# Converting a second weight matrix later inside a fused mLSTM and Fourier-mix kernel

## The chip, the cores and the metric

The kernel runs on one core of one Trainium2 chip. The metric is the device time of one execution in microseconds (us), lower is better. Three runs of the kernel before gave a median of 402.24 us (402.18 to 402.57). One execution was also profiled; every duration below comes from that one.

## What is computed

An mLSTM cell runs over 4 batches, 8 heads, 768 tokens and 40 features a head. Its output, reshaped to (4, 768, 320), goes through a Fourier mix and a two-layer MLP:

```python
for t in range(S):                       # attention part
    m_new = np.maximum(f_gate[:, :, t] + m, i_gate[:, :, t])
    ...
    C = f_stab * C + i_stab * np.einsum('bhd,bhe->bhde', vt, kt)
    h_tilde = np.einsum('bhde,bhe->bhd', C, qt)
    ...
    y[:, :, t] = o * h_tilde / denom
X = np.fft.fft(np.fft.fft(x, axis=1), axis=2)    # second part, x = y reshaped
u = x + np.real(X)
un = (u - mu) / np.sqrt(var + 1e-06)
ch = np.maximum(un @ w_ch1, 0.0) @ w_ch2          # 320 -> 1280 -> 320
return u + ch
```

The two weight matrices arrive as 64-bit floats. The kernel reads them as 64-bit words and turns them into 32-bit floats by itself, and that conversion is what the change moves.

## The kernel before, in words

**Order of the work.** The whole program is laid out by hand in numbered slots. `at(slot, phase, fn, ...)` puts a call into a plan, and `run` (line 127) emits the calls sorted by slot and phase. Within a slot the phases are EVAC = 0, FILL = 1, MAIN = 2 and FILL_PE = 3, with fractions for the order inside one. A slot is not a stretch of time that the chip knows: it only fixes the order in which each engine gets its instructions. Each engine works through its own instructions in that order and waits, where it must, for another engine's result.

**Batches.** Four batches overlap (lines 1331 to 1335). While batch 0 is in its MLP (`mlp_in`, slots 31 to 50, the first layer; `mlp_out`, slots 51 to 62, the second), batch 1 is in its recurrence (`plan_halves`, line 762). That recurrence has six chunks of 128 tokens. Chunk c starts at slot 32 + 3c, so a period of the recurrence is three slots. The text calls a step of it by batch and chunk, as in (1,2).

**A chunk of the recurrence**, with s = 32 + 3c (lines 762 to 788):
- ScalarE: exponentials of half the heads (`mlstm_exp`, line 491) in slot s-1 and the other half in slot s
- TensorE, slot s: scores (`halves_scores`) and the sums for the state (`halves_to_state`) into one PSUM bank pair, which has a single copy
- VectorE: `halves_add` (lines 665, 667), the state's two halves, in slots s+1 and s+2 ahead of everything else there; `halves_weigh` (line 672) in slot s+1. Both read the bank pair, so the next chunk's scores wait for them
- GpSimd: `halves_decay` (line 652), the scaled queries (line 501), the mask (line 515), the weighted values (line 507)
- TensorE, slot s+3: `halves_from_state`, then `halves_from_chunk` with turn 0, and after the next chunk's scores `halves_from_chunk` with turn 1. Between the two turns ScalarE makes a one-element copy, `halves_between` (line 699, tile `warm`), for which turn 1 waits
- VectorE, slot s+4: `mlstm_finish` (lines 712 to 720).

**A piece of the weights** (class `Piece`, lines 382 to 427) is 128 x 640 numbers. There are ten, n = 0 to 9: 0 to 4 are the first matrix, 5 to 9 the second. Each goes through four steps: `load` (line 396, 640 KB on SyncE's queue into tile `raw`, two buffers), `take` (lines 406 and 408, VectorE, tiles `e` and `m`, one buffer each), `convert` (lines 413 and 414, ScalarE, two instructions) and `join` (lines 420, 422 and 426, VectorE). The load of piece n waits for the join of piece n-2, the take of n for the join of n-1. Lines 1342 to 1351 put the steps into the plan: each triple in `when` is the slot and phase of take, convert and join.

**Who needs the pieces.** `mlp_in` for blocks 4 and 5 (slots 35 and 36) is the first to read pieces 3 and 4. `mlp_out` reads pieces 5 to 7 in slot 51 and pieces 7 to 9 in slot 52. `weight_sums` (line 1081) reuses the tiles `raw`, `e` and `m` from slot 52 on.

**Other work in these slots.** `mix_add` (line 937) on VectorE adds the Fourier part for batch 0 (slots 31, 35, 36), `mix_center` (line 971, tile `uc`) and `mix_turn_out` (line 983) on ScalarE follow it, with TensorE's transposes (line 978, tile `put`) between them. After every second block of `mlp_in`, ScalarE runs two `mlp_relu` (line 1071).

The steps of pieces 3 to 9 stand in these slots before:

| piece | take | convert | join |
|---|---|---|---|
| 3 | 22 | 23 | 27 |
| 4 | 27 | 28 | 32 |
| 5 | 33 | 34 | 34 |
| 6 | 34 | 35 (after TensorE's work of the slot) | 36 |
| 7 | 36 | 37 | 38 |
| 8 | 39 | 40 | 41 |
| 9 | 42 | 43 | 44 |

Of the kernel before, what the change touches and what calls it, by code (L numbers as in the profile page):

```python
# [53 lines left out]
def kernel(  # L54
# [1285 lines left out]
    at(60, FILL + 0.4, lambda: nc.gpsimd.memset(ds_sb[0:1, 0, 0, :], 1.0))  # L1340

    when = [((2, 0.7), (4, 0.5), (6, 0.6)), ((6, 0.7), (7, 0.5), (8, 0.6)), ((11, 0.7), (13, 0.5), (22, 0.6))]
    when += [((22, 0.7), (23, 0.7), (27, 0.6)), ((27, 0.7), (28, 0.7), (32, 0.6))]
    when += [((33, 0.7), (34, 0.3), (34, 0.6)), ((34, 0.7), (35, 2.7), (36, 0.6))]
    when += [((s, 0.7), (s + 1, 0.7), (s + 2, 0.6)) for s in (36, 39, 42)]
    pieces = w1_pieces + w2_pieces
    for n, (w, p) in enumerate(zip(when, pieces)):
        if n > 4:
# [138 lines left out]
```

## Time and profile before

| what | value |
|---|---|
| median of three runs | 402.24 us |
| the profiled execution's own time | 402.53 us |
| its span in the trace | 400.8 us |
| TensorE busy (matmul) | 382.8 us, 96% |
| VectorE busy | 279.8 us, 70% |
| ScalarE busy | 171.7 us, 43% |
| GpSimd busy | 132.6 us, 33% |
| mean granted TensorE clock | 0.991 |

The span is what the trace covers; the other 1.73 us of the profiled execution lie around it. In the trace's names PE is TensorE's matmuls, PEld its weight loads, DVE VectorE, ACT ScalarE, POOL GpSimd and SP SyncE, whose queue issues the transfers. A timeline line gives start, duration, engine, line of the kernel, operation, names of what is written and read, shapes and count; a bracket at its end is the idle time of that engine just before and what ended it. In this program a float matmul leaves two records, so `x8` on line 1056 is four matmuls of the first layer.

The matmuls of `mlp_in` begin at 59.18 us, those of `mlp_out` at 117.65 us. The stretch between them is where slots 31 to 50 run.

### The profile page before, as it was taken

The page shows a single profiled execution, that of the slowest core. Times are in us where ns is not written, and L with a number is a line of the kernel's source. Part 1 is how long each engine was busy: PE and PEld are TensorE (multiplying, and loading weights), DVE is VectorE, ACT ScalarE, POOL GpSimd, SP SyncE. Part 2 cuts the span into 40 slices and gives each one's busy share as a digit, 9 for nine tenths or more (in the row PEclk, how much of TensorE's full clock was granted, in tenths as well). Part 3 has the DMA queues.
Part 4 walks back from the last instruction along what each step waited for, and adds up shares of the span by engine and source line. Part 5 has one row for each costly group of instructions (what it writes and reads, how often), then busy time and mean ns, then how long its engine had stood idle before and what let it go on. Part 6 is the DMA issues. An engine that isn't in the chain of part 4 may idle for free.

```text
span 400.8 us, 10588 instructions
## 1 busy us (share of the span) xinstructions
PE 382.8 (96%) x4174; PEld 278.4 (69%) x4174; DVE 279.8 (70%) x671; ACT 171.7 (43%) x481; POOL 132.6 (33%) x237
## 2 busy tenths in 40 slices
PE   8999899979999999998999989989999999999996
PEld 6877555545567677755569888845578986556996
DVE  7789988999665467485775598777764686336652
ACT  6987367655640232655462214544440023454000
POOL 5648513555863341253255124451310000020000
PEclk9999999979999999999999999999999999999999
DMA  7878499677286254447800526410000000000100
GB/s 222 288 228 246 151 241 275 191 191 220 72 190 169 60 155 127 118 133 185 186 1 28 138 71 194 145 38 2 0 0 18 17 34 33 2 0 0 34 33 34
DMA packets 25631, 44.78 MB, mean 112 GB/s; under 512 B 5727, under 2 KB 14766, under 8 KB 25454
## 3 DMA queue, kind: packets, MB, share of 16 engines
q1 hardware_dynamic: 25582, 44.11, 39.1%
q8 instruction: 33, 0.54, 0.6%
q14 instruction: 16, 0.13, 0.1%
HBM read 38.49 MB, written 4.12 MB: 106 GB/s over the span
## 4 chain that ended last, share of the span: by engine, by line
PE 67%; DVE 18%; DMA 6%; issue 4%; ACT 2%; POOL 1%; SPq 1%; DVEq 0%; POOLq 0%; ACTq 0%
PE po L1237 18%; PE pm L1118 14%; PE po L1181 8%; PE pm L1056 5%; PE ph L519 4%; PE pm L1123 4%; PE pu L935 3%; PE ps L519 2%; DMA Gb<-G_d 2%; DVE so L716 2%; DMA raw<-in_w 1%; PE pz L904 1%; PE pz L892 1%; DMA W<-M_d 1%; PE put L978 1%
## 5 line engine op out<-in xcount | busy, mean ns | idle before, releaser
L1187 DVE SCALAR_TENSOR_TENSOR x<-po,rstd,x 128x160 f32<-128x160 f32 (+1 forms) x69 | 27.0, 395 | 43.9 <-PE po L1237 36.8
L1127 DVE TENSOR_TENSOR h<-h,pm 128x384 f32<-128x384 f32 x60 | 30.5, 550 | 29.2 <-PE pm L1123 13.9
L652 POOL TENSOR_TENSOR C<-C,decB 128x164 f32<-128x164 f32 x30 | 16.0, 532 | 75.7 <-DVE C L667 64.7
L1118 PE MATMUL pm<-uT,w_sb 128*128 128x384 f32 x90 | 37.7, 506 | 2.1 <-DVE h L1127 1.3
L491 ACT ACTIVATE W<-W,colT 128x64 f32<-128x64 f32 x144 | 37.4, 339 | 0.0
L1181 PE MATMUL po<-w_sb,h 128*128 128x320 f32 x120 | 34.2, 435 | 0.0
L1056 PE MATMUL pm<-uT,w_sb 128*128 128x384 f32 x80 | 31.2, 528 | 0.3 <-DVE x L955 0.2
L515 POOL TENSOR_SCALAR_AFFINE_SELECT W<-W 64x512 f32<-64x512 f32 x36 | 27.2, 756 | 11.7 <-ACT W L491 10.4
L1002 POOL TENSOR_TENSOR t<-rstd 128x6 f32<-128x6 f32 x12 | 3.4, 281 | 81.9 <-DVE v L996 81.4
L1237 PE MATMUL po<-T,S 128*128 128x160 f32 x180 | 27.9, 302 | 1.5 <-DVE x L1187 1.5
L501 POOL TENSOR_TENSOR qg<-qk,Gb 128x512 f32<-128x512 f32 (+1 forms) x21 | 28.7, 1368 | 1.4 <-DMA kvt<-in_kv 0.8
L1181 PEld LDWEIGHTS po<-w_sb,h 128*128 128x128 f32 x120 | 22.3, 190 | 9.5 <-issue 0.6
L1237 PEld LDWEIGHTS po<-T,S 128*128 128x128 f32 x180 | 25.5, 190 | 3.2 <-DVE x L1187 2.0
L1118 PEld LDWEIGHTS pm<-uT,w_sb 128*128 128x128 f32 x90 | 15.5, 189 | 16.4 <-DVE h L1127 7.5
L1237 PE MATMUL po<-w_sb,h 128*128 128x160 f32 x180 | 26.3, 300 | 0.0
L1237 PEld LDWEIGHTS po<-w_sb,h 128*128 128x128 f32 x180 | 25.2, 190 | 1.4 <-DVE x L1187 0.3
L1174 ACT ACTIVATE h<-h 128x384 f32<-128x384 f32 x45 | 23.1, 520 | 2.0 <-DVE h L1127 2.0
L1123 PE MATMUL pm<-uT,w1t_sb 64*128 64x384 f32 x120 | 23.4, 508 | 0.0
L983 ACT COPY uT<-put 128x384 f32<-128x384 f32 x24 | 11.1, 476 | 27.5 <-PE put L978 27.5
L1056 PEld LDWEIGHTS pm<-uT,w_sb 128*128 128x128 f32 x80 | 15.0, 202 | 11.0 <-issue 3.2
L507 POOL TENSOR_TENSOR vw<-kvt,colT 128x328 f32<-128x328 f32 x23 | 18.0, 782 | 12.7 <-DVE colT L360 10.1
L971 ACT ACTIVATE uc<-x 128x384 f32<-128x384 f32 x24 | 14.4, 613 | 18.1 <-DVE x L963 12.1
(241 smaller groups left out, 843.3 us busy)
## 6 DMA issues: line engine op xcount, KB each, us to landing
kvt<-in_kv SPq DMA_DIRECT2D x24, 336.0 KB
qk<-in_qkT SPq DMA_DIRECT2D x48, 160.0 KB
raw<-in_w SPq DMA_DIRECT2D x10, 640.0 KB
Gb<-G_d SPq DMA_DIRECT2D x36, 128.0 KB
W<-M_d SPq DMA_DIRECT2D x36, 128.0 KB
so<-in_o SPq DMA_DIRECT2D x24, 160.0 KB
out<-x SPq DMA_DIRECT2D x24, 160.0 KB
x<-so SPq DMA_DIRECT2D x9, 140.0 KB
```

The lines of the kernel that those rows point to most:

```text
L491: nc.scalar.activation(out=k.W[:, h, :], in_=M, func=AF.Exp, scale=-1.0, bias=colT[:, c, 0, b * H + h:b * H + h + 1])
L501: nc.gpsimd.tensor_tensor(out=k.qg[:, :, t], in0=k.qk[:, 0, :, t], in1=k.Gb[:, :, t], op=OP.mult)
L515: nc.gpsimd.affine_select(out=W, in_=W, compare_op=OP.is_ge, fill=0.0, base=base, pattern=[[0, H], [step, LH]], channel_multiplier=-1)
L519: nc.tensor.matmul(out, w, x, start=start, stop=True, skip_group_check=True)
L1056: nc.tensor.matmul(k.pm[i], w1_sb[:, ch, f0:f0 + L], u[2 * ch], start=(ch == 0 and not ahead), stop=(ch == 1 and ahead), skip_group_check= ...
L1118: nc.tensor.matmul(bank, w, u, start=start, stop=True, skip_group_check=True)
L1123: nc.tensor.matmul(bank, block(w1t_sb, i)[rows], mlp_u(gr, 1)[rows], start=False, stop=True, skip_group_check=True)
L1127: nc.vector.tensor_tensor(out=h, in0=h, in1=bank, op=OP.add)
L1174: nc.scalar.activation(out=h, in_=h, func=AF.Relu, scale=-1.0)
L1181: nc.tensor.matmul(k.po, hidden(gr, f)[:, i * L:(i + 1) * L], w2_sb[:, f, :], start=(f == 0), stop=(f == NFF - 1))
L1187: nc.vector.scalar_tensor_tensor(out=u, in0=po, scalar=k.rstd[:, c:c + 1], in1=u, op0=OP.mult, op1=OP.add)
L1237: nc.tensor.matmul(po, a[:, f], w[:, f], start=start and f == 0, stop=f == half - 1, skip_group_check=True)
```

## The change

Only the table `when` changes. Piece 3 is joined in slot 31 and no longer in 27. With it piece 4 moves: it is taken in slot 31, converted in 32 and joined in 33. Pieces 5 to 9 follow at three-slot steps, from slots 36, 39, 42, 45 and 48, each with its convert one slot and its join two slots after the take. The last join is now in slot 50 and no longer in 44. The loads of pieces 5 to 9 move too, since line 1349 puts the load of piece n one slot after the join of piece n-2: from slots 28, 33, 35, 37, 39 to 32, 34, 39, 42, 45. No instruction is added or taken away.

```diff
     when = [((2, 0.7), (4, 0.5), (6, 0.6)), ((6, 0.7), (7, 0.5), (8, 0.6)), ((11, 0.7), (13, 0.5), (22, 0.6))]
-    when += [((22, 0.7), (23, 0.7), (27, 0.6)), ((27, 0.7), (28, 0.7), (32, 0.6))]
-    when += [((33, 0.7), (34, 0.3), (34, 0.6)), ((34, 0.7), (35, 2.7), (36, 0.6))]
-    when += [((s, 0.7), (s + 1, 0.7), (s + 2, 0.6)) for s in (36, 39, 42)]
+    when += [((22, 0.7), (23, 0.7), (31, 0.5)), ((31, 0.7), (32, 0.7), (33, 0.6))]
+    when += [((s, 0.7), (s + 1, 0.7), (s + 2, 0.6)) for s in (36, 39, 42, 45, 48)]
     pieces = w1_pieces + w2_pieces
     for n, (w, p) in enumerate(zip(when, pieces)):
         if n > 4:
             at(when[n - 2][2][0] + 1, FILL + 0.7, p.load)
         for (s, phase), fn in zip(w, (p.take, p.convert, p.join)):
             at(s, FILL + phase, fn)
```

## The prediction

> **What bounds the kernel now.** I read the page's slices first. TensorE is busy nearly everywhere, and its granted clock falls in one slice of ten us only, the ninth (80 to 90 us).
>
> ```profile
> PE   8999899979999999998999989989999999999996
> PEclk9999999979999999999999999999999999999999
> ```
>
> Next I read the list of waits of TensorE between 56 and 125 us, the stretch in which pieces 3 to 9 are handled. It is short: 3.6 us in four waits (columns: total, times, longest).
>
> ```profile
> PE ps L519 <- DVE C L667: 1.9, 1, 1.9
> PE ph L519 <- ACT warm L699: 1.1, 1, 1.1
> PE put L978 <- ACT uc L971: 0.4, 1, 0.4
> PE pm L1056 <- DVE x L955: 0.2, 1, 0.2
> ```
>
> TensorE's timeline places the two long ones, and shows that the first layer's next eight records take 4.63 us where the same group takes 2.85 us at 99.20:
>
> ```profile
> 83.82 0.69 PE L519 MATMUL ps<-qk 40*64 40x64 f32 x32 [1.86 <-DVE C L667]
> 84.33 0.70 PE L519 MATMUL ps<-vw,kvt 64*40 64x41 f32 x32
> 86.17 0.66 PE L519 MATMUL ph<-kvt,W 64*64 64x41 f32 x16 [1.13 <-ACT warm L699]
> 86.76 0.90 PE L978 MATMUL put<-ident,uc 128*128 128x128 f32 x3
> 87.46 4.63 PE L1056 MATMUL pm<-uT,w_sb 128*128 128x384 f32 x8
> ...
> 99.20 2.85 PE L1056 MATMUL pm<-uT,w_sb 128*128 128x384 f32 x8
> ```
>
> The table of windows says why (the clock is the 0.50 ahead of the DMA share): after the waits the clock is halved until about 91.1 us.
>
> ```profile
> 83.00:84.00 1.00, 0.18 (x11) 0.18 (x14) 0.76 (x3) 0.84 (x2) 0.16 (x1) 1.00 0.57 113
> 88.00:89.00 1.00, 1.00 (x3) 0.60 (x2) 0.66 (x4) 1.00 (x4) 0.92 (x2) 0.50 0.77 232
> ```
>
> Last, the chain of work that ended last, in order of time, names what TensorE waited for. The join of piece 6 and the take of piece 7 run ahead of the state's add on VectorE, and the convert of piece 7 runs ahead of the exponentials and `warm` on ScalarE:
>
> ```profile
> 80.27 0.73 DVE e L420
> ...
> 81.78 0.84 DVE w_sb L426
> ...
> 82.64 0.50 DVE e L406
> ...
> 83.16 0.43 ACT e L413
> ...
> 83.90 0.72 ACT m L414
> 84.62 0.95 ACT W L491 x4
> ...
> 86.08 0.05 ACT warm L699
> ```
>
> So this spot is bound by the weights' conversion on VectorE and ScalarE; from 87.46 to 126 us TensorE has no wait at all, though VectorE idles there only about 6 us in all, the longest being:
>
> ```profile
> 105.59 0.33 DVE L667 TENSOR_TENSOR C<-C,ps 128x164 f32<-128x164 f32 x1 [1.72 <-POOL C L652]
> 111.95 0.33 DVE L667 TENSOR_TENSOR C<-C,ps 128x164 f32<-128x164 f32 x1 [2.74 <-PE ps L519]
> ```
>
> **What the Trainium skill says.** "TensorE: Matmul & The Clock Gate", Part 1, has the clock drop to half after an idle window of about 3.4 us and return after a busy one. The trace agrees roughly: 1.86 and 1.13 us of waiting, with some 1.2 us of work between, and then 0.50 for about 6.7 us. "GPSIMD Engine Reference", section 8, says that GpSimd shares SBUF interfaces with VectorE and contends with its two-input instructions. The trace agrees: line 422 takes 0.82 us at 80.92 with GpSimd idle and 1.88 us at 84.91 under GpSimd's line 501.
>
> **The change, part by part.** Times named "before" are starts in the trace.
>
> *Slots 27 to 36, VectorE.* From 57.91 (join 3) to 83.45 (the late add) VectorE runs four joins and four takes; after the change joins 3 and 4 and takes 4 and 5. What leaves is joins 5 and 6 (0.81 + 1.08 + 1.77 and 0.81 + 0.82 + 0.82) and takes 5 and 6 (0.57 + 1.02 and 0.83 + 0.94): 9.5 us, and a 1.32 us wait for a transfer. Joins 3 and 4 come later but in time: batch 0's add of slot 31 goes first (58.0 to 59.15), join 3 ends near 61.6, take 4 near 62.4, and join 4, behind its convert and the first add of (1,0), near 66.9. Blocks 4 and 5 read those pieces at 70.95 and 74.96, so 4 us or more cover it.
>
> *ScalarE there.* With take 4 at 61.6 the exponentials of (1,0) run first and `uc` at about 64.4 instead of 65.86, so TensorE's 0.44 us wait for `put` at 66.52 goes. VectorE now waits for TensorE: the add of (1,1) follows at about 74.4 (before 75.89), and the 3.70 us from there to the weigh (75.89 to 79.59) put that at 78.1. The 0.16 us wait at 77.45 goes too.
>
> *Slots 36 to 38.* After the weigh (0.60) comes take 5 (0.81), then the second add, done at 79.8. TensorE wants it at 81.95 - 0.6 = 81.35: the 1.86 us go with 1.5 us to spare. ScalarE's convert 5 runs 79.1 to 80.5, exponentials to 81.5, `uc` to 82.05, `warm` at 82.15; turn 1 wants it at 82.3. The 1.13 us go, with almost nothing to spare. No idle, no halved clock: 4.63 becomes 2.85 (1.8), and the transposes and small products at half clock give about 0.7 (0.90, 0.66 and 0.70 against 0.55, 0.42 and 0.50). Sum: 0.44 + 0.16 + 1.86 + 1.13 + 1.8 + 0.7 = 6.1 us, all on TensorE's path.
>
> *Slots 39 to 50, where it is given back.* Here come joins 6, 7, 8 and takes 7, 8, 9 in place of joins 8, 9 and take 9 (join 9 falls at the end). VectorE keeps the old spacing: weigh to weigh was 10.94 us with join 6 in it. Less that join (2.45) and its waits of 0.26 and 0.47 it is 7.76, so the weigh of (1,2) is at 85.9. From there to that of (1,4) was 90.53 to 108.29 = 17.76 with two pieces in it; less the 0.37 us wait for TensorE that is 17.4, so 103.2. TensorE asks for it at 110.75 - 6.1 = 104.65: in time. But take 8 follows it (103.8), convert 8 waits for take 8 (104.3 to 105.7), and behind convert 8 on ScalarE stand two `mlp_relu` (0.8), four exponentials (1.0) and `warm` (0.1): 107.6. Turn 1 of (1,4) wants that at 111.63 - 6.1 = 105.5. A new wait of 2.1 us. It is between 1.2 (take 8 without contention and a join 0.5 shorter) and 3.0 (take 8 as slow as take 6, 1.77).
>
> *Slot 50 on.* Join 8 starts near 105.3 and takes 2.45 to 3.96 (the joins of 101.45 and 92.51); with add 0.25 and finish 1.65 to 2.05 the weigh of (1,5) ends at 110.3 to 112.2. TensorE wants it at 115.24 - 4.0 = 111.2: 0 to 1.0, I take 0.2. Join 9 follows the fold of slot 50 (1.6, from 114.89 to 116.5 before) and ends at 116 to 117.5; block 8 of `mlp_out` reads it at 117.65 - 3.8 + 2.69 + 1.6 = 118.1. Covered by 0.6 us or more; if not, it costs what it is late. VectorE's 3.09 us idle at 123.43 then takes up its lag.
>
> *Loads.* Each still waits on SyncE's queue for a join, with exponent inputs and `so` behind it. Load 5 waits for join 3 (about 61), load 7 for join 5 (about 83). Each lands well before its take, some 10 us later; before, take 5 waited 1.32 us. Cost zero; if the cover failed, about 1.3 us a piece.
>
> Sum: -6.1 + 2.1 + 0.2 = -3.8 us. The profiled execution of 402.53 us (span 400.8 and 1.73 around it) goes to 398.7; it lies 0.29 above the median, so the median of 402.24 goes to **398.4**.
>
> **Rivals.** (1) *Nothing comes back*: GpSimd leaves VectorE alone, take 8 is done before 101.7, `warm` is in time: -6.1, 396.1 us. For it: GpSimd is 33% busy. Against: the 8.7 us old spacing, and GpSimd's chain ahead of the add at 105.59.
> (2) *More comes back*: the 2.1 us wait joins the scores' wait in slot 47 and the clock halves again, 1.8 to 2 us: 400.4. For it: 3.0 us of waiting did it before. Against: 2.1 is shorter.
> (3) *Slower: VectorE becomes the bound of slots 39 to 50.* The weigh of (1,5) is at 78.1 plus four periods P. Before it was in time at 114.3, with 0.3 to spare, so beyond P = 9.1 us the kernel loses. I have P = 8.1. With joins and takes stretched by GpSimd throughout as the worst were (line 422 1.89, line 426 1.77, take 1.77), P nears 9.5: 78.1 + 38.0 = 116.1, 1.5 us late, and the halved clock 1.8: 405.5. Against: the two measured periods with a whole piece were 8.73 and 9.03, waits included.
> (4) *No net effect*: another result is late at 81.35 and the old wait stays under a new name; 402.2. Against: GpSimd's results for (1,1) were there in time.
>
> **How the numbers follow.** About 0.2% (0.8 us) is what a measurement can tell from no change. Forecast (397.2 to 399.8) 0.50; (1) 0.15; (2) 0.20; (4) 0.05; (3) 0.10. Faster: 0.50 + 0.15 + 0.20 = 0.85; same 0.05; slower 0.10. The range 396.2 to 401.2 takes in the forecast, (2) and half of (1), about 0.8.
>
> **What would show it.** Right: no waits near 82 to 86, the clock whole in the ninth slice, first layer's eight records 2.85 us there; a wait for `warm` of about 2 us in slot 47, near 106; `mlp_out` starting near 113.9 instead of 117.65, and the same 3.8 us at the end. Wrong: a clock below 1 between 80 and 125, a wait for a weigh (line 672) or join (line 426) over 1 us, or a later gap that takes back what `mlp_out`'s start gained.

## The result and the profile after

| what | before | after |
|---|---|---|
| median of five runs | 402.24 us | 400.46 us |
| the profiled execution's own time | 402.53 us | 400.47 us |
| its span | 400.8 us | 398.8 us |
| start of `mlp_in`, of `mlp_out` in the trace | 59.18, 117.65 us | 59.48, 115.50 us |
| ratio after to before, 95% interval | | 0.9943 [0.9923, 0.9963] |

By the medians the kernel is 1.78 us faster; the forecast was 3.8. The ratio is one of means and stands for 2.3 us, between 1.5 and 3.1. (Two runs further down, of the changed kernel once more and of the last experiment, each had one execution of 542 us at a mean clock of 0.66, which their ratios leave out.) The page's slices show that the dip of the clock has not gone: it has moved, from the ninth slice to the twelfth, and is shallower.

```profile
PE   8999899999899999998999989989999999999996
PEclk9999999999989999999999999999999999999999
```

The list of TensorE's waits between 56 and 125 us is down from 3.6 to 2.5 us (columns: total, times, longest):

```profile
PE ph L519 <- ACT warm L699: 2.2, 2, 1.7
PE put L978 <- ACT uc L971: 0.3, 1, 0.3
```

TensorE's timeline places them. In slot 38 a small rest of the old waits is left and the eight records that took 4.63 us take 2.75. In slot 47 there is a new wait, and behind it eight records of the same kind take 4.54 us, where before they took 2.85 (at 111.98):

```profile
82.42 0.44 PE L519 MATMUL ph<-kvt,W 64*64 64x41 f32 x16 [0.50 <-ACT warm L699]
...
83.18 2.75 PE L1056 MATMUL pm<-uT,w_sb 128*128 128x384 f32 x8
...
107.76 0.44 PE L519 MATMUL ph<-kvt,W 64*64 64x41 f32 x16 [1.74 <-ACT warm L699]
108.13 4.54 PE L1056 MATMUL pm<-uT,w_sb 128*128 128x384 f32 x8
```

The table of windows gives the granted clock there, again the figure ahead of the DMA share. It is whole until 109 and then 0.50 until past 112.

```profile
106.00:107.00 1.00, 0.02 (x4) 0.00 (x0) 1.00 (x2) 1.00 (x4) 1.00 (x2) 1.00 0.03 5
110.00:111.00 1.00, 1.00 (x3) 0.66 (x2) 0.96 (x2) 0.00 (x0) 0.79 (x3) 0.50 0.92 203
```

The chain of work that ended last, in order of time, runs through the same kinds of steps as before the change, now with piece 8: the weigh of (1,4), take 8, convert 8, the rectifiers, the exponentials and the one-element copy.

```profile
102.92 0.69 DVE W L672
103.62 0.88 DVE e L406
...
104.52 0.76 ACT e L413
...
105.88 0.85 ACT h L1071 x2
106.73 0.95 ACT W L491 x4
107.67 0.04 ACT warm L699
```

Two intervals of the traces give the balance. From the start of `mlp_in` to the tail matmuls of block 9 (92.02 before, 85.85 after) TensorE gained 32.84 - 26.37 = 6.5 us. From there to the start of `mlp_out` it lost 29.65 - 25.63 = 4.0 us. Of that, 2.1 us lie between the state product of (1,4) and turn 1 (1.36 us before, 3.48 after), 1.7 us in the halved clock (4.54 against 2.85), and 0.2 us are spread over the stretch before slot 47. What is left, 2.45 us, is 2.15 us in the trace's own times because `mlp_in` began 0.30 us later. That start lies anywhere between 58.54 and 60.13 us in the traces of this case, with no order by the change.

### The profile page after: what moved, and what is told of

Read it like the earlier page. It is cut to its first block, busy times and chain, and to the rows that moved or that the text cites. A ratio compares the mean times of both kernels' runs of the same rounds, so it can differ in the third digit from the quotient of the medians.

```text
span 398.8 us, 10582 instructions
## 1 busy us (share of the span) xinstructions
PE 382.2 (96%) x4174; PEld 278.0 (70%) x4174; DVE 279.4 (70%) x671; ACT 171.8 (43%) x481; POOL 134.6 (34%) x237
## 4 chain that ended last, share of the span: by engine, by line
PE 66%; DVE 17%; DMA 6%; issue 4%; ACT 3%; POOL 2%; SPq 1%; DVEq 0%; POOLq 0%; ACTq 0%
PE po L1237 18%; PE pm L1118 14%; PE po L1181 8%; PE pm L1056 3%; PE pm L1123 3%; PE pu L935 3%; PE ph L519 3%; PE ps L519 2%; DMA kvt<-in_kv 2%; PE put L978 2%; DMA Gb<-G_d 1%; DMA raw<-in_w 1%; PE pz L904 1%; PE pz L892 1%; DMA qk<-in_qkT 1%
## 5 line engine op out<-in xcount | busy, mean ns | idle before, releaser
L501 POOL TENSOR_TENSOR qg<-qk,Gb 128x512 f32<-128x512 f32 (+1 forms) x21 | 27.6, 1316 | 0.1
L507 POOL TENSOR_TENSOR vw<-kvt,colT 128x328 f32<-128x328 f32 x23 | 18.9, 820 | 13.0 <-DVE colT L360 10.1
```

Source lines behind the costliest of these rows:

```text
L501: nc.gpsimd.tensor_tensor(out=k.qg[:, :, t], in0=k.qk[:, 0, :, t], in1=k.Gb[:, :, t], op=OP.mult)
```

## The experiments

The theory: the gain is real, and what came back comes from VectorE's work of the weights, now crowded into slots 39 to 50, through the take and convert that stand in front of the copy `warm`. There are three rivals: VectorE is simply too slow there; or GpSimd's chain in front of VectorE's add is the cause; or the joins of pieces 3 and 4 made the gain. The edits below are made to the changed kernel, unless they say otherwise. Each ratio is to the kernel before, run beside it. The changed kernel itself, run once more, gave this:

> The changed kernel itself once more, beside the two others on the same chip. Both theories: ratio to before 0.993 to 0.997; the wait for the one-element copy in slot 47 at 1.6 to 1.9 us. It settles how much of the difference to the other runs lies in the chip.

Measured: 0.9929 [0.9903, 0.9955], 400.42 us, the wait in slot 47 at 1.7 us. The first measurement holds.

**Each part alone.** First only pieces 5 to 9 moved, then only pieces 3 and 4:

```diff
-    when += [((22, 0.7), (23, 0.7), (31, 0.5)), ((31, 0.7), (32, 0.7), (33, 0.6))]
+    when += [((22, 0.7), (23, 0.7), (27, 0.6)), ((27, 0.7), (28, 0.7), (32, 0.6))]
```

> Only pieces 5 to 9 stand as in the changed kernel; pieces 3 and 4 stand as before the change. Theory (the waits near 82 and 86 went because pieces 5 and 6 left slots 33 to 36): both stay away, the wait for the transposed block of 0.4 us near 66 comes back, the wait in slot 47 stays as in the changed kernel: 400.5 to 401.0. Rival (pieces 3 and 4 matter, they let the additions of batch 0 run first): a wait for the state's add near 82 comes back, 402 or more.

Measured: 0.9953 [0.9935, 0.9970], 401.16 us. The wait near 82 stays away and the one near 86 is down to 0.49 us; the 0.4 us for the transposed block is back; the wait in slot 47 is 1.74 us. This is as the theory had it; the median lies 0.16 us above its range.

```diff
-    when += [((s, 0.7), (s + 1, 0.7), (s + 2, 0.6)) for s in (36, 39, 42, 45, 48)]
+    when += [((33, 0.7), (34, 0.3), (34, 0.6)), ((34, 0.7), (35, 2.7), (36, 0.6))]
+    when += [((s, 0.7), (s + 1, 0.7), (s + 2, 0.6)) for s in (36, 39, 42)]
```

> Only pieces 3 and 4 stand as in the changed kernel (joins in slots 31 and 33); pieces 5 to 9 stand as before the change, so that slots 31 to 36 hold joins 3 to 6 and takes 4 to 7. Theory (the gain comes from pieces 5 and 6 leaving those slots): VectorE is as late at the state's second add of (1,1) as before, the waits near 82 and 86 and the halved clock stay: ratio to before 0.998 to 1.003. Rival (joining 3 and 4 later is what helps): the waits near 82 are gone, ratio about 0.990.

Measured: 1.0028 [1.0014, 1.0041]: slower than before. Its list of waits has the two long old ones again:

```profile
PE ps L519 <- DVE C L667: 1.9, 1, 1.9
PE ph L519 <- ACT warm L699: 1.3, 1, 1.3
PE put L978 <- ACT uc L971: 1.1, 1, 1.1
```

The 1.1 us for the transposed block lies at 76.69; a wait of 0.8 us stands at the same block, at 77.74, in the trace of the kernel before with a later Newton step (below). So the gain belongs to pieces 5 and 6 leaving slots 33 to 36. Joining 3 and 4 later without that costs a little. The likely reason is that it adds to the crowd, but the trace, of one of the fastest of 22 executions, does not show it.

**Taking one step out of the chain to the copy.** Convert 8 behind the copy:

```diff
+    when[8] = ((45, 0.7), (47, 2.65), (48, 0.6))
```

> Convert 8 moves on ScalarE from slot 46 to slot 47 behind the one-element copy, join 8 to slot 48; nothing else moves. Theory (the 1.74 us wait of TensorE in slot 47 comes from convert 8, which waits for take 8 and holds back the rectifiers, exponentials and the copy): that wait is under 0.4 us, the clock stays whole, the second layer starts near 112.0 instead of 115.5; join 9 then ends near 117.5 and block 8 of the second layer may wait 1 to 1.5 us for it, so 1.9 to 3.5 us less than the changed kernel: 397.0 to 398.5. Rival (VectorE as a whole is too slow in slots 39 to 50, whatever stands on ScalarE): a wait of about the same size turns up in slots 47 to 50 for the weigh, 400 to 401.

Measured: 0.9942 [0.9926, 0.9957]. The wait in slot 47 is gone, as the theory says, but the time is not better: convert 9, which waits for take 9, stands in front of the copy of slot 50.

```profile
113.82 0.53 PE L519 MATMUL ph<-kvt,W 64*64 64x41 f32 x16 [2.25 <-ACT warm L699]
```

That copy is hardly later than in the changed kernel (54.3 us after the start of `mlp_in`, there 54.2). There TensorE, held up in slot 47, reached it late; here it comes early and waits. The clock halves behind this wait, and the first 30 records of `mlp_out` take 9.89 us instead of 8.34.

Take 8 ahead of the weigh, right behind join 7:

```diff
+    when[8] = ((44, 0.7), (46, 0.7), (47, 0.6))
```

> Only take 8 moves, from slot 45 behind the weigh of (1,4) to slot 44 right behind join 7, into the 1.73 us in which VectorE idles for GpSimd. Theory: convert 8 is then ready before the rectifiers need ScalarE, TensorE's wait for the copy in slot 47 goes, the clock stays whole; join 8 still stands ahead of the weigh of (1,5), for which TensorE may wait up to 1 us in slot 50: 397.0 to 398.8. Rival (VectorE too slow as a whole): the wait moves to the weigh of (1,5) in full and the clock halves anyway, 400 to 401.

Measured: 0.9938 [0.9925, 0.9952], no more than the changed kernel. The wait in slot 47 is gone; in slot 50 TensorE waits for VectorE's finish and weigh, and the clock halves there:

```profile
109.78 0.98 PE L519 MATMUL ph<-C,qg 40*64 40x41 f32 x32 [1.01 <-DVE x L720]
111.12 0.44 PE L519 MATMUL ph<-kvt,W 64*64 64x41 f32 x16 [0.36 <-DVE W L672]
```

VectorE is not full in front of them. It idles first for GpSimd's decay, which stands behind a Newton step, and then for GpSimd's mask:

```profile
107.57 0.33 DVE L667 TENSOR_TENSOR C<-C,ps 128x164 f32<-128x164 f32 x1 [0.83 <-POOL C L652]
110.38 0.69 DVE L672 TENSOR_TENSOR W<-ps,W 128x512 f32<-128x512 f32 x1 [0.74 <-POOL W L515]
```

In both runs the named step did cause the named wait, and in both my expectation of the time was wrong. The rival was right that the wait only wanders; its reason, a VectorE without room, does not fit the second trace, where GpSimd holds VectorE up.

**Fewer pieces in the crowded slots.** The changed kernel leaves VectorE idle for 2.21 and 2.64 us in slots 34 and 35 (at 70.70 and 74.57). Piece 5 goes there and the rest moves up:

```diff
-    when += [((s, 0.7), (s + 1, 0.7), (s + 2, 0.6)) for s in (36, 39, 42, 45, 48)]
+    when += [((34, 0.7), (35, 0.3), (35, 0.6))]
+    when += [((s, 0.7), (s + 1, 0.7), (s + 2, 0.6)) for s in (36, 39, 42, 45)]
```

> Piece 5 in the idle of slots 34 and 35, the other four in the regular steps from slots 36, 39, 42 and 45, so that the regular steps hold four pieces and end in slot 47. Theory: the take and convert that stand in slots 45 and 46 (now those of piece 9) still come ahead of the one-element copy in slot 47, so the 1.7 us wait and the halved clock stay there; slots 48 to 50 are free of weights, which brings at most 0.5 us: ratio 0.991 to 0.994. Rival (one piece less in slots 39 to 50 is enough by itself): the wait in slot 47 is gone, ratio under 0.989.

Measured: 0.9951 [0.9939, 0.9964], the wait in slot 47 unchanged at 1.74 us. The wait is as the theory had it; the ratio lies just outside its range. One piece less at the end does not help while the take of slot 45 and the convert of slot 46 stay where they are.

The same with the last piece taken in slot 44 and joined in 48:

```diff
+    when += [((s, 0.7), (s + 1, 0.7), (s + 2, 0.6)) for s in (36, 39, 42)] + [((44, 0.7), (46, 0.7), (48, 0.6))]
```

> Piece 5 goes into the 4.9 us in which VectorE idles in slots 34 and 35 of the changed kernel (take 34, convert and join 35), pieces 6 to 8 to the places of 5 to 7 (slots 36, 39, 42), piece 9 is taken in slot 44 behind join 8, converted in 46 and joined in 48 behind the weigh; nothing of the weights is left in slots 49 and 50. Theory (what came back is VectorE's work crowded into slots 39 to 50, whose waits only wander when one step is moved): no wait over 0.6 us between 60 and 125, clock whole, the second layer starts near 112, ratio to before 0.984 to 0.988. Rival (the crowding is not the cause, some other result is as late): a wait of over 1 us in slots 47 to 50 all the same, ratio 0.992 to 0.995.

Measured: 0.9904 [0.9884, 0.9924], 398.57 us: better, less than expected. In the trace, take 9 waited for its transfer and then ran beside GpSimd's queries and mask, which stretched line 406 from 0.48 to 2.54 us; the finish of (1,3) came late, and with it TensorE's state product of (1,4) in slot 47. (The trace puts that wait down to a GpSimd step that ended at the same moment. The product writes the PSUM tile that the finish reads, and it starts 0.15 us after the finish ends, at 104.93. In the run with take 8 early, where the trace names the finish itself, the product of the next chunk starts 0.15 us after it too.) The profiled execution is the slowest of the six and the only one with a mean clock below 0.999.

```profile
99.12 2.54 DVE L406 TENSOR_SCALAR e<-raw 128x640 uint32<-128x640 uint32 x1 [1.34 <-DMA raw<-in_w]
```

**GpSimd's chain.** In the changed kernel VectorE idles 1.73 us, until 100.22, for GpSimd's decay, which stands behind GpSimd's first Newton step for batch 0. The chain of work shown above also runs through that decay, ahead of the weigh at 102.92:

```profile
99.74 0.45 POOL C L652
...
102.10 0.81 POOL W L515
```

So the step is moved one slot later:

```diff
-            at(s + 3 * n if b == 0 else s, FILL + 0.65, mix_rstd_step, b)
+            at(*((s + 1, FILL + 0.45) if b == n == 0 else (s + 3 * n if b == 0 else s, FILL + 0.65)), mix_rstd_step, b)
```

> The changed kernel with GpSimd's first Newton step for batch 0 moved from slot 43 to slot 44 behind the state's decay and the scaled queries of (1,4). Theory (the 1.73 us that VectorE idles in front of the add of (1,4) is bought with GpSimd's absence: the scaled queries then run beside join 7, and line 422 takes 1.9 instead of 0.82): take 8 comes at most 0.6 us earlier, the wait in slot 47 is still over 1 us, ratio 0.993 to 0.996. Rival (GpSimd's chain in front of that add is the cause of the wait): the wait in slot 47 is under 0.4 us, the clock stays whole, ratio about 0.987.

Measured: 0.9891 [0.9872, 0.9911], 397.76 us. My theory failed here: I had expected contention to eat the gain. Part of it was eaten, but elsewhere: beside GpSimd's queries the small VectorE instruction of line 994 took 1.21 us instead of 0.17. The queries end (97.12) as join 7 begins (97.14), and line 422 stays at 0.81 us. Take 8 comes 0.96 us earlier counted from the start of `mlp_in`, the wait in slot 47 falls from 1.74 to 0.96 us, and the clock stays whole:

```profile
106.27 0.44 PE L519 MATMUL ph<-kvt,W 64*64 64x41 f32 x16 [0.96 <-ACT warm L699]
106.64 2.85 PE L1056 MATMUL pm<-uT,w_sb 128*128 128x384 f32 x8
```

The rival was right about the cause and its ratio was nearly met, though the wait did not vanish: at 0.96 us it is near the size that my theory gave it. Most of the gain is the clock: the wait is 0.8 us shorter, the eight records are back from 4.54 to 2.85 us, and all five executions have a mean clock of 0.999 or 1.000. The same edit on the kernel before:

> The kernel before the change, with only the first Newton step moved to slot 44 as in the earlier run on the changed kernel. Theory (that step costs time only where VectorE has no slack left behind it; before the change the 1.72 us wait ahead of the add of (1,4) was followed by no wait of TensorE): ratio 0.998 to 1.002. Rival (the Newton step costs by itself): ratio 0.994 or less.

Measured: 0.9988 [0.9975, 1.0002], no change. So the Newton step does not cost by itself; that it costs where VectorE has no slack behind it fits both runs.

**The clock.** Four idle products were added to slot 47, in front of turn 1 (with them the kernel no longer computes the right values; they write into the bank of that chunk's sums, in other columns, and how they disturb it was not traced):

```diff
+    at(47, FILL_PE + 2.7, fill, 4)
```

> The changed kernel with four extra matmuls (zeros, 256 columns, into unused PSUM columns) on TensorE in slot 47 between the state's sums and turn 1, about 1.7 us of activity in place of the 1.74 us of idle; nothing reads them. Theory (the wait halves the clock afterwards, which costs the 1.7 us by which the first layer's eight records took 4.54 instead of 2.85): the turn comes no earlier, but the clock stays whole, 398.5 to 398.9. Rival (the small matmuls ahead of it, or something else, lower the clock): the eight records still take about 4.5 us, 400.4 or a little more.

Measured: 0.9959 [0.9944, 0.9973], 400.79 us. It didn't do what it was meant to: the products, too, waited for the copy, so they ran behind the wait and not in its place.

```profile
108.41 1.99 PE L1373 MATMUL ph<-rest 128*128 128x256 f32 x8 [1.74 <-ACT warm L699]
...
110.70 2.85 PE L1056 MATMUL pm<-uT,w_sb 128*128 128x384 f32 x8
```

Still it says something: the eight records take 2.85 us after the same 1.74 us of idle, and 1.99 us of extra work cost only what the halved clock had cost. Five of six executions had a mean clock of 1.000. In the executions of the changed kernel it was never whole. So the length of the wait alone does not decide whether the clock halves.

**Both delays removed.** Piece 5 in the idle, piece 9 taken in slot 44 and joined in 48, and all three Newton steps one slot later:

```diff
-            at(s + 3 * n if b == 0 else s, FILL + 0.65, mix_rstd_step, b)
+            at(*((s + 3 * n + 1, FILL + 0.45) if b == 0 else (s, FILL + 0.65)), mix_rstd_step, b)
```

> Piece 5 in the idle of slots 34 and 35, piece 9 taken in slot 44 and joined in 48 as in the run before, and in addition all three Newton steps of batch 0 one slot later on GpSimd, behind the decay and the scaled queries (slots 44, 47, 50). Theory (what came back is two delays of VectorE's chain ahead of the weigh of (1,4): the take and convert in front of the one-element copy, and the wait for GpSimd's decay behind its Newton step): both are gone, no wait of TensorE over 0.8 us between 60 and 125, the clock whole in most runs, ratio to before 0.983 to 0.987. Rival (take 9, slowed to 2.5 us and more by GpSimd and late by its transfer, keeps the chain as late): a wait over 1 us in slot 47 stays, ratio 0.988 to 0.992.

Measured: 0.9847 [0.9818, 0.9876], 396.94 us, the best of all. Its list of waits between 56 and 125 us has one entry, its clock shows no dip, and `mlp_out` starts 52.4 us after `mlp_in` (before 58.5, after the change 56.0):

```profile
PE ph L519 <- ACT warm L699: 0.7, 1, 0.7
```

```profile
PEclk9999999999999999999999999999999999999999
...
111.47 8.34 PE L1181 MATMUL po<-w_sb,h 128*128 128x320 f32 x30
```

That is 6.0 us less than before, about the 6.1 us which the first half of the prediction's sum had found, kept to the end. Three edits stand together here. The Newton step alone gave 0.9891 and the moved pieces alone 0.9904, and what each adds to the other was not taken apart further.

## Why the prediction was right, and where its size was off

- **The relief of slots 33 to 38** was sized right: 6.1 us forecast, 6.5 measured. Part of the agreement is luck: 0.50 us of the wait for the copy stayed, where I had it just in time, and the waits that went had cost more than their listed idle. From turn 0 to the scores it was 2.29 us before (81.53 to 83.82) and 0.23 after, which is 2.06 for a wait of 1.86. The two runs with one part each show that it belongs to pieces 5 and 6.
- **VectorE's pace** was right. I put the weighs of (1,2) and (1,4) at 85.9 and 103.2; they started at 86.09 and 102.92 in a trace that runs 0.30 us later. The four periods were 7.80, 7.80, 9.03 and 8.14 us, mean 8.2; I had 8.1, and 9.1 as the point beyond which the kernel loses. Rival (3) was not reached. One reading was off: VectorE's 6 us of idle are those from 87.46 to the start of `mlp_out`; up to 126 us it is 10, with 3.09 the longest.
- **The new wait in slot 47** was right in place, cause and size: the copy was to be done at 107.6 and was done at 107.70; TensorE came 2.1 us later, as forecast. The 0.2 us for the weigh of (1,5) agrees by luck: that weigh ended at 111.74, and TensorE, held up by the clock, asked for it only at 113.09. The 0.2 us that the trace has lie before slot 47.
- **The term that was mis-sized is the clock.** "Sum: -6.1 + 2.1 + 0.2" gave the new wait no clock penalty; I kept it for rival (2), and held against it that "2.1 is shorter" than the 3.0 us of before. The profile after has 1.7 us of it. With it the sum is -6.5 + 2.1 + 1.7 + 0.2 = -2.5 us in the traces' intervals; the means give -2.3 and the medians -1.8. Rival (2), 400.4 us, is what happened. The forecast's own span, 397.2 to 399.8, was missed; the wider range holds because it took rival (2) in. And the first sign of being wrong that I had named, a clock below 1 between 80 and 125, did come. All ten executions of the changed kernel that the comparisons use had a mean clock of 0.995 or 0.996.
- **Why I mis-sized it**: I read the dip before the change as the work of both waits, 1.86 and 1.13 us. Finer windows of the trace before show that the clock fell at 84.4, after the first wait (it ended at 83.82) and ahead of the second (85.0 to 86.2):

```profile
82.50:84.40 1.90, 0.58 (x40) 0.58 (x44) 1.61 (x5) 1.24 (x2) 0.56 (x2) 1.00 0.83 162
84.40:91.20 6.80, 5.67 (x65) 3.73 (x56) 6.19 (x11) 4.28 (x15) 5.19 (x5) 0.50 0.91 252
```

So the wait to compare with was 1.86 us, and the 2.1 us of the forecast are longer. Both it and the 1.74 us after the change are about half of the idle window of 3.4 us that the prediction took from the Trainium skill, "TensorE: Matmul & The Clock Gate", Part 1; here the measurement decides. Around both waits stand small products, 40 or 64 rows by 41 to 64 columns, before the 1.74 us for another 1.7 us. That such products count less for the clock than the first layer's full ones would fit, but no run here separates it. The same part says that the window in which activity is judged runs freely, so that the moment varies from run to run. The traces agree: the wait in slot 47 ends at 107.76, 107.60 and 107.76 us in the changed kernel, in its second run and in the run with only piece 5 in the idle, and the clock halves from 109.0, 108.1 and 108.4.

- **The loads and join 9** cost nothing, as forecast; join 9 ended at 118.2 instead of 116 to 117.5 because line 422 took 2.51 us, and block 8 of `mlp_out`, near 119.8, still found it ready. That, too, is partly luck: without the halved clock block 8 would have come 1.7 us earlier, near 118.1, level with the join. When piece 9's take was pulled forward, the transfer did become late, by 1.34 us, so the cover would have been thin there.

What stays open is what exactly decides whether a gap of 1.7 us halves the clock.

## What to carry to other kernels

Work that moves out of a crowded stretch lands in another: before it is moved, find the engine's idle time (here 4.9 us in slots 34 and 35) and consider putting it there, not at an even spacing. That alone brought nothing here (0.9951); it was part of the best version, together with an earlier last take and GpSimd's steps moved. Where an engine is nearly full, one step moved only makes the wait wander, so look at what else stands in front of the late result, on other engines too. And price a new TensorE wait with the clock it may cost, not with its length alone.

## What the hardware showed that was not expected

The clock's dip is partly chance. The run with piece 5 in the idle time was executed 22 times: in 9 executions the mean clock was 0.999 or 1.000, with a mean time of 399.5 us; in 13 it was 0.994 to 0.996, with a mean of 400.8 us. It is the same program, with 1.3 us between the two groups. In every trace with a dip the halved stretch lasts 3.4 us (109.0 to 112.5 after the change) or twice that (84.4 to 91.2 before). The kernel before had mean clocks of 0.991 or 0.992 in 59 of the 83 executions that ran beside the experiments and of 0.996 in 23. The two traces at 0.991 and 0.992 have the long dip and all at 0.995 or 0.996 the short one, so the length of the dip before is chance as well.

And one-input VectorE instructions can be slowed beside GpSimd as well, by more than the prediction allowed a take: line 406 took 0.48 us alone and 2.54 us beside GpSimd's scaled queries and mask, and line 994 took 0.17 and 1.21 us. Section 8 of "GPSIMD Engine Reference" in the Trainium skill, which the prediction cites, names VectorE's instructions in a 2-port mode besides those with two inputs; the traces do not show which mode these two lines run in.
